# Transposing the states' exponentials by 32 by 32 blocks and a DMA instead of on TensorE, in a fused attention and SwiGLU kernel

## The chip, the cores and the metric

The kernel runs on one core of one Trainium2 chip. The metric is the device time of one execution in microseconds (us). Engines are named as the profile names them: PE is TensorE (PEld its weight loads), DVE is VectorE, ACT is ScalarE, POOL is GpSimd, SP is SyncE, whose queue issues nearly all DMAs.

## The reference, cut to what matters (softmax written short)

There are 8 batches of 8 heads; each head has 512 tokens and 32 states of width 64. Tokens read states and states read tokens, both with a softmax. All 544 rows of a batch, 512 wide over the heads, then go through an RMS norm and a SwiGLU layer of 1536 units.

```python
scores = scale * np.matmul(x, state.transpose(0, 1, 3, 2))      # 512 x 32
a = softmax(scores)                ; xread = np.matmul(a, state)
scores2 = scale * np.matmul(state, x.transpose(0, 1, 3, 2))     # 32 x 512
a2 = softmax(scores2)              ; sread = np.matmul(a2, x)
x = np.concatenate([xread, sread], axis=2)     # then (B*S, H*D) = (4352, 512)
rms = np.sqrt(np.mean(x * x, axis=-1, keepdims=True) + 1e-06)
xn = x / rms * rms_g
g = xn @ w_gate ; val = xn @ w_val
out = (g / (1 + np.exp(-g)) * val) @ w_out
```

## The kernel before, in words

Everything is float32. The kernel works batch by batch in a software pipeline. After an opening stage (batch 0, the reading of batch 1, the conversion of the weights) come seven periods, one for each of the batches 1 to 7, and a last stage for the 256 state rows of all batches.

A period does two things at once. It runs the SwiGLU layer for the 512 tokens of batch b: the hidden products (`hidden_seven`, line 674, each product in seven instead of eight block products) and the output products (`project_seven`, line 836). And it runs the attention of batch b + 1: `tokens_read` and `states_read`. The order within a period is written out by hand for PE, DVE and ACT: a string `PERIOD` has one letter for each step, a letter stands for a stream (a Python generator), and each letter emits that stream's next step. `h` are the hidden products on PE, `t` and `u` what ACT and DVE do with them; `p`, `c` and `k` are the output products, their copies by ACT and sums by DVE; `v`, `w` and `x` make the batch's own weights (line 528 on PE, ACT copies, POOL sums); `a` is `tokens_read`, `s` is `states_read`. Each engine runs its instructions in the order of the string; waits between engines follow from the data. The same string serves all seven periods. In the last, where there is no further batch, `s` is empty and `a` stands for the norm of the state rows. POOL's and SP's orders are not written by hand.

The steps that the change touches, in the order of a batch:

- `tokens_read` multiplies the softmaxed scores by the states (line 410, PE), ACT squares the four results into `sq`, three DVE additions (line 420) leave one tile `sq[:, 0]` of 128 partitions by 512 tokens. PE sums it over partitions with four products against a column of ones (line 424), DVE adds 1e-6 (line 428), POOL takes the power -0.5 (line 270), PE spreads the result along rows (line 277), DVE scales the batch's `aT_s` with it (line 434). The scaled `aT_s` and POOL's `slot_sums` of it are what the next period's first hidden products read.
- `states_read` takes the maximum of the states' scores (line 446, DVE), ACT makes the exponentials `e2` and their sums (line 452), PE transposes them in two groups of four 128 by 128 blocks (line 459), ACT copies each group from PSUM to `e2T` (line 461), and PE multiplies `e2T` with the batch's tokens (line 471). DVE divides by the sums (line 478), PE transposes the result (line 482), DVE puts it into `xsT` (line 484), which only the last stage reads.

From batch 2 on the scores themselves are already made on blocks: DVE transposes 32 by 32 blocks of the inputs (lines 329 and 335) and `x` is loaded so that this suffices. A block transpose exchanges rows and columns inside each 32 by 32 block and leaves every block within its own 32 partitions.

Three pools of PSUM tiles matter: `aps` (two buffers, named `at` in the profile) holds nearly everything of the attention, `vps` (two, `pv`) shares the own weights' products, and `fx`, `fy`, `fz` (`f`) belong to the layer's products. The tag `eS` is one SBUF buffer, held by the tokens' exponentials during the first part of a batch.

Of the kernel before, what the change touches and what calls it, by code (L numbers as in the profile page):

```python
# [8 lines left out]
F32 = mybir.dt.float32  # L9
# [3 lines left out]
ALU = mybir.AluOpType  # L13
ACTF = mybir.ActivationFunctionType
AXX = mybir.AxisListType.X
PSUM = bass.MemoryType.PSUM

P = 128
# [10 lines left out]
)  # L29

PERIOD = (
    "hhtvtvhtxhuxhuthhtuhuhtxhhhutuuuhthhuttxahhxhthuuuuuxhavuvhtxhtxhhttuauhxuxhxuut"
    "hhhtuhthutuuhuuuhhauuhtaaauxuhthautuuhhthuhuautaaphuuuapuaaaaacaasapcpaaaaaaaakp"
    "psackaauaacakkpapaakaacpsaskcsssppsasspwswkswxkxxkkpxpxccxss"
)

STATES = (
# [6 lines left out]
def kernel(  # L44
# [20 lines left out]
    nc = tc.nc  # L65
    VE, SE, GE, TE = nc.vector, nc.scalar, nc.gpsimd, nc.tensor
# [75 lines left out]
    GE.memset(bounds[:, 1:2], 255.0 * (1 << 23))  # L142
    rms_g = consts.tile([P, NI], F32, name="rms_g")


    w_d = [scratch.tile([P, NI, 2, 2, P], F32, name="w_d%d" % mp) for mp in range(NM // 2)]
    w_sb = {}
    wo = consts.tile([P, NM, DM], F32, name="wo")
    hb = consts.tile([P, NM, S], F32, name="hb")
# [117 lines left out]
    def mean_root(ss, n):  # L267

        ri = two.tile([P, NC], F32, name="ri")
        GE.tensor_tensor(out=ri[:, 0:n], in0=ss, in1=mhalf[:, 0:n], op=ALU.pow)  # L270
        return ri

    def along_rows(ri, n):

        rp = aps.tile([P, NC, P], F32, name="at")
        for c in range(n):
            TE.transpose(out=rp[:, c, :], in_=ri[:, c:c + 1].to_broadcast([P, P]), identity=ident)  # L277
        return rp.rearrange("p c t -> p (c t)")
# [4 lines left out]
    def scores(b, packed, soft):  # L283

        xb = x_sb[b]
        stT = two.tile([P, 4, Ns], F32, name="stT")
        tp = aps.tile([P, 4, Ns], F32, name="at")
        TE.transpose(out=tp.rearrange("p j n -> p (j n)"),
                     in_=packed.rearrange("p e d -> p (e d)"), identity=ident)
        yield  # L290
        VE.tensor_copy(stT, tp)
        yield "step"

        xT = one.tile([P, 4, NC, P], F32, name="xT", tag="xT")
        for c in range(NC):
            tp = aps.tile([P, 4, P], F32, name="at")
            for j in range(4):
                TE.transpose(out=tp[:, j, :], in_=xb[:, c, P * j:P * j + P], identity=ident)
            yield
            SE.copy(xT[:, :, c, :], tp)  # L300
            yield "step"


        sp = [aps.tile([P, S], F32, name="at") for e in range(2)]
        for j in range(4):
            for e in range(2):
                TE.matmul(out=sp[e][Ns * j:Ns * j + Ns, :], lhsT=stT[D * e:D * e + D, j, :],
                          rhs=xT[D * e:D * e + D, j].rearrange("p c t -> p (c t)"),
                          start=True, stop=True)
        yield  # L310


        sS = read[b] = two.tile([P, 2, NC, P], F32, name="sS")
        eS = soft["e"] = one.tile([P, 2, S // Ns, Ns], F32, name="eS", tag="eS")
        for e in range(2):
            VE.transpose(out=eS[:, e].rearrange("p k n -> p (k n)"), in_=sp[e])
            yield
            SE.copy(sS[:, e].rearrange("p c t -> p (c t)"), sp[e])
            yield "step" if e else None

        soft["st"] = stT
        soft["half"] = lambda e: eS[:, e]
        soft["back"] = lambda e: [(aT_s[b][:, e], eS[:, e].rearrange("p k n -> p (k n)"))]

    def scores_of_blocks(b, packed, soft):
# [30 lines left out]
        for g in (2, 3, 0, 1):  # L356
# [7 lines left out]
                                   eS[:, g].rearrange("p e c n -> p e (c n)"))  # L364
                                  for g in (2 * q, 2 * q + 1)]

    def tokens_read(b):
        packed, soft = rows.pop(b), {}
        yield from (scores if b < 2 else scores_of_blocks)(b, packed, soft)
        half = soft["half"]  # L370
        m1 = two.tile([P, 2, S // Ns], F32, name="m1")
        z1 = two.tile([P, 2, S // Ns], F32, name="z1")

        def along(t, e):
            return t[:, e].unsqueeze(2).to_broadcast([P, S // Ns, Ns])

        for e in range(2):
            VE.reduce_max(out=m1[:, e], in_=half(e), axis=AXX)
            yield
            VE.tensor_tensor(out=half(e), in0=half(e), in1=along(m1, e), op=ALU.subtract)  # L380
            yield
            SE.activation(out=half(e), in_=half(e), func=ACTF.Exp, scale=SCALE)
            yield "step"
        stT_g[b] = two.tile([P, 4, Ns], F32, name="stT_g")
        if b > 1:
            soft["st"] = aps.tile([P, 4, Ns], F32, name="at")
            TE.transpose(out=soft["st"].rearrange("p j n -> p (j n)"),
                         in_=packed.rearrange("p e d -> p (e d)"), identity=ident)
            yield
        VE.tensor_tensor(out=stT_g[b], in0=soft["st"], in1=rms_g.unsqueeze(2).to_broadcast([P, 4, Ns]),  # L390
                         op=ALU.mult)
        yield
        aT_s[b] = two.tile([P, 2, S], F32, name="aT_s")
        for e in range(2):
            VE.reduce_sum(out=z1[:, e], in_=half(e), axis=AXX)
            yield
            VE.tensor_scalar(z1[:, e], z1[:, e], 1e-9, None, op0=ALU.add)
            VE.reciprocal(z1[:, e], z1[:, e])
            yield
            VE.tensor_tensor(out=half(e), in0=half(e), in1=along(z1, e), op=ALU.mult)  # L400
            yield
            for to, blocks in soft["back"](e):
                VE.transpose(out=to, in_=blocks)
            yield "step"


        reads = [(aps, vps)[j // 2].tile([P, S], F32, name=("at", "pv")[j // 2]) for j in range(4)]
        for j in range(4):
            for e in range(2):
                TE.matmul(out=reads[j][D * e:D * e + D, :],  # L410
                          lhsT=packed[Ns * j:Ns * j + Ns, e, :],
                          rhs=aT_s[b][Ns * j:Ns * j + Ns, e],
                          start=True, stop=True)
        yield
        sq = one.tile([P, 4, S], F32, name="sq", tag="xT")
        for i, j in enumerate((2, 3, 0, 1)):
            SE.activation(out=sq[:, i, :], in_=reads[j], func=ACTF.Square, scale=DM ** -0.5)
            yield "step" if i == 3 else None
        for i, j in ((0, 1), (2, 3), (0, 2)):
            VE.tensor_tensor(out=sq[:, i, :], in0=sq[:, i, :], in1=sq[:, j, :], op=ALU.add)  # L420
            yield
        sp = aps.tile([P, NC], F32, name="at")
        for c in range(NC):
            TE.matmul(out=sp[:, c:c + 1], lhsT=sq[:, 0, P * c:P * c + P], rhs=ones,  # L424
                      start=True, stop=True)
        yield
        ss = two.tile([P, NC], F32, name="ss")
        VE.tensor_scalar(ss, sp, 1e-6, None, op0=ALU.add)
        yield "step"
        ri = mean_root(ss, NC)  # L430
        yield
        rp = along_rows(ri, NC)
        yield
        VE.tensor_tensor(out=aT_s[b], in0=aT_s[b],
                         in1=rp.unsqueeze(1).to_broadcast([P, 2, S]), op=ALU.mult)
        yield "step"

    def states_read(b):

        xb, sS = x_sb.pop(b), read.pop(b)  # L440
        e2 = one.tile([P, 2, NC, P], F32, name="e2")
        s2 = two.tile([P, 2], F32, name="s2")
        m2 = two.tile([P, 2], F32, name="m2")
        z2 = two.tile([P, 2], F32, name="z2")
# [4 lines left out]
        VE.tensor_scalar(s2, m2, -SCALE, None, op0=ALU.mult)  # L449
        yield  # L450
        for e in range(2):
            SE.activation(out=e2[:, e], in_=sS[:, e], func=ACTF.Exp, scale=SCALE,
                          bias=s2[:, e:e + 1], accum_out=z2[:, e:e + 1])
            yield "step" if e else None
        e2T = one.tile([P, 2, NC, P], F32, name="e2T")
        for e in range(2):
            tp = aps.tile([P, NC, P], F32, name="at")
            for c in range(NC):
                TE.transpose(out=tp[:, c, :], in_=e2[:, e, c, :], identity=ident)  # L459
            yield  # L460
            SE.copy(e2T[:, e], tp)
            yield "step"
        VE.tensor_scalar(z2, z2, 1e-9, None, op0=ALU.add)
        VE.reciprocal(z2, z2)
        yield
# [1 line left out]
        for e in range(2):  # L467
            for c in range(NC):
                for j in range(4):
                    h = 2 * j + e  # L470
                    TE.matmul(out=rp[Ns * j:Ns * j + Ns, e, :],  # L471
                              lhsT=e2T[:, e, c, Ns * j:Ns * j + Ns],
                              rhs=xb[:, c, D * h:D * h + D],
                              start=(c == 0), stop=(c == NC - 1))
        yield
# [567 lines left out]
```

## Time and profile before

| what | value |
|---|---|
| median of 5 runs (lowest to highest) | 791.63 us (790.94 to 792.32) |
| the profiled execution: its time, its span | 791.63 us, 789.8 us |
| granted TensorE clock in it | 0.998 |
| PE busy, PEld busy | 777.7 us (98%), 604.4 us (77%) |
| DVE, ACT, POOL busy | 521.7 us (66%), 334.4 us (42%), 170.8 us (22%) |
| DMA moved | 95.77 MB, mean 121 GB/s |

The profile is of one execution, whose time is also the median; 1.8 us of it lie around the span. A period, from one batch's first hidden product to the next one's, takes 85.48 us (223.83 to 309.31 us of the trace). Busy shares are means over stages with different limits. PE's busy time counts pipelined matmuls, so a busy PE is not PE at its peak; how much one matmul costs in a row of them is read from the chain of waits, where its share of the time stands without overlap.

### The profile page before, as it was taken

The numbers are of one execution on the slowest core, as the hardware profiler recorded it, in microseconds if no ns is written. First come the engines' busy times: TensorE is split into PE (matmuls) and PEld (weight loads), VectorE is DVE, ScalarE is ACT, GpSimd is POOL, SyncE is SP. The second block draws the span as 40 slices with busy tenths as digits, with TensorE's granted clock in tenths as the row PEclk, the third lists the DMA queues.
The fourth block names the chain that finished last, engine by engine and source line by source line (L and its number), as shares of the span: only waits on it lengthen the run. The fifth ranks groups of instructions, "written<-read, shape, count | busy, mean of one in ns | idle before, by whom it ended". The sixth has DMA issues, their size and how long they took to land.

```text
span 789.8 us, 13559 instructions
## 1 busy us (share of the span) xinstructions
PE 777.7 (98%) x5478; PEld 604.4 (77%) x5478; DVE 521.7 (66%) x822; ACT 334.4 (42%) x560; POOL 170.8 (22%) x216
## 2 busy tenths in 40 slices
PE   6999999999999999999999999999999999999998
PEld 5643444788878887888878887888788887888996
DVE  4999997688338951887268833895189725781461
ACT  5998864552245323542255124532353225410320
POOL 0100003430244023420433024402341043400000
PEclk9999999999999999999999999999999999999999
DMA  9888865730065005610263007500530024201311
GB/s 286 228 271 311 275 190 167 217 122 1 24 203 217 2 17 177 221 31 17 90 217 121 1 24 207 215 2 14 197 153 12 13 79 176 107 5 35 121 54 27
DMA packets 69277, 95.77 MB, mean 121 GB/s; under 512 B 46432, under 2 KB 54112, under 8 KB 62304
## 3 DMA queue, kind: packets, MB, share of 16 engines
q1 hardware_dynamic: 67040, 94.33, 36.5%
q8 instruction: 43, 0.70, 0.4%
q10 hardware_dynamic: 2176, 0.59, 0.4%
q14 instruction: 18, 0.15, 0.1%
HBM read 79.69 MB, written 15.20 MB: 120 GB/s over the span
## 4 chain that ended last, share of the span: by engine, by line
PE 93%; DVE 5%; issue 0%; DMA 0%; ACT 0%; SPq 0%
PE f L674 37%; PE f L836 35%; PE f L776 5%; PE pv L570 4%; PE at L528 3%; PE pv L528 3%; DVE ex L248 1%; PE at L471 1%; PE at L410 1%; DVE raw L244 1%; PE at L346 1%; PE at L424 1%; PE at L459 1%; DVE w_m L253 1%; PE pv L346 1%; PE at L277 0%
## 5 line engine op out<-in xcount | busy, mean ns | idle before, releaser
L836 PE MATMUL f<-wo,hb 128*128 128x256 f32 x540 | 123.4, 380 | 0.2 <-ACT ot L873 0.2
L674 PE MATMUL f<-aT_s,v 128*128 128x256 f32 x504 | 120.6, 382 | 0.0
L836 PEld LDWEIGHTS f<-wo,hb 128*128 128x128 f32 x540 | 101.4, 190 | 13.5 <-ACT ot L873 0.4
L674 PEld LDWEIGHTS f<-aT_s,v 128*128 128x128 f32 x504 | 94.1, 190 | 19.6 <-DVE c L736 5.0
L736 DVE TENSOR_TENSOR g<-g,f 128x512 f32<-128x512 f32 (+1 forms) x96 | 61.9, 653 | 68.4 <-PE f L674 63.9
L674 PE MATMUL f<-aT_t,vs 128*128 128x256 f32 x336 | 87.1, 381 | 0.0
L270 POOL TENSOR_TENSOR ri<-ss,mhalf 128x4 f32<-128x4 f32 x8 | 13.5, 1692 | 321.2 <-DVE s L449 210.9
L727 ACT ACTIVATE hb<-g 128x1024 f32<-128x1024 f32 (+1 forms) x48 | 48.2, 1005 | 79.3 <-DVE g L736 79.3
L836 PE MATMUL f<-wt,hs 128*128 128x256 f32 x360 | 81.0, 381 | 0.0
L836 PEld LDWEIGHTS f<-wt,hs 128*128 128x128 f32 x360 | 67.3, 190 | 14.1 <-issue 5.1
L674 PEld LDWEIGHTS f<-aT_t,vs 128*128 128x128 f32 x336 | 63.2, 190 | 15.0 <-issue 5.9
L873 ACT COPY ot<-f 128x256 f32<-128x256 f32 x60 | 21.4, 373 | 122.9 <-PE f L836 122.9
L554 POOL TENSOR_TENSOR vs<-v 128x256 f32<-128x256 f32 x42 | 31.4, 746 | 164.3 <-ACT v L539 164.2
L739 DVE SCALAR_TENSOR_TENSOR hb<-hb,g 128x1024 f32<-128x1024 f32 x42 | 53.2, 1267 | 4.6 <-ACT hb L727 4.6
L725 ACT COPY g<-f 128x512 f32<-128x512 f32 (+1 forms) x48 | 26.9, 561 | 55.8 <-PE f L674 55.8
L776 PE MATMUL f<-wo,hb 128*128 128x512 f32 x96 | 44.7, 600 | 0.0
L557 POOL TENSOR_TENSOR vs<-v,vs 128x256 f32<-128x256 f32 x42 | 44.4, 1056 | 0.0
L570 PE MATMUL pv<-aT_s,v 128*128 128x512 f32 x96 | 43.6, 593 | 0.0
L674 PE MATMUL f<-aT_s,vs 128*128 128x256 f32 x168 | 43.1, 379 | 0.0
L674 PE MATMUL f<-aT_t,v 128*128 128x256 f32 x168 | 43.1, 379 | 0.0
L836 PE MATMUL f<-wo,hs 128*128 128x256 f32 x180 | 41.2, 379 | 0.0
L836 PEld LDWEIGHTS f<-wt,hb 128*128 128x128 f32 x180 | 33.7, 190 | 9.4 <-DVE ot L881 5.0
(144 smaller groups left out, 1279.8 us busy)
## 6 DMA issues: line engine op xcount, KB each, us to landing
w_m<-w_d SPq DMA_DIRECT2D x48, 1024.0 KB, 6.5
out_dram<-ot SPq DMA_DIRECT2D x56, 128.0 KB, 2.1
raw<-in_moe_w_val_dram SPq DMA_DIRECT2D x6, 1024.0 KB, 5.5
raw<-in_moe_w_out_dram SPq DMA_DIRECT2D x6, 1024.0 KB, 7.9
x_b<-in_x_dram SPq DMA_DIRECT2D x96, 64.0 KB, 2.6
w_d<-w_m SPq DMA_DIRECT2D x6, 1024.0 KB, 4.9
raw<-in_moe_w_gate_dram SPq DMA_DIRECT2D x5, 1024.0 KB, 6.9
x_b<-in_x_dram SPq DMA_DIRECT2D x6, 256.0 KB, 6.7
```

The costliest lines, as they stand in the source:

```text
L528: TE.matmul(out=pv[e][Ns * j:Ns * j + Ns, :], lhsT=stT_g[b][D * e:D * e + D, j, :], rhs=w[D * e:D * e + D, j].rearrange("p m k f -> p (m k ...
L554: GE.tensor_tensor(out=vs[:, 0], in0=a21, in1=a22, op=ALU.add)
L557: GE.tensor_tensor(out=vs[:, 2], in0=a12, in1=vs[:, 1], op=ALU.subtract)
L570: TE.matmul(out=to[0], lhsT=lhs(i, k), rhs=r, start=(i == 0), stop=(i == len(rhs) - 1))
L674: TE.matmul(out=ps[:, i, 0:half], lhsT=l[:, i, :], rhs=r, start=(start and i == 0 and k == 0), stop=(k == len(lhs) - 1), skip_group_check= ...
L725: SE.copy(gates(q)[1], q["x"][:, :, 0:half])
L727: SE.activation(out=hb[:, 2 * mp:2 * mp + 2, 0:n].rearrange("p m (c t) -> p m c t", c=2), in_=q["g"][:, :, :, 0:half], func=ACTF.Silu if s ...
L736: VE.tensor_tensor(out=to, in0=to, in1=q[ps][:, :, 0:half], op=ALU.add)
L739: VE.scalar_tensor_tensor(out=h, in0=h, scalar=1.0, op0=ALU.add, op1=ALU.mult, in1=q["g"].rearrange("p m c t -> p m (c t)"))
L776: TE.matmul(out=banks[r], lhsT=hb[:, m, P * r:P * r + P], rhs=wo[:, m, :], start=(m == 0), stop=(m == NM - 1))
L836: TE.matmul(out=banks[name][:, r, :], lhsT=lhs(k)[:, P * r:P * r + P], rhs=rhs(k), start=(start and r == 0 and k == 0), stop=(k == HM - 1) ...
L873: SE.copy(to, banks[name][:, r, :])
```

## The change

For batches 0 and 1 the arithmetic and its order stay. For batches 2 to 7:

- `states_read`: the two groups of TensorE transposes and the two ACT copies go. ACT writes the exponentials in another layout, DVE transposes all of them by 32 by 32 blocks in one instruction into `eB` (which takes the buffer with tag `eS`), a DMA from ScalarE's queue writes `eB` to a scratch tensor in HBM (512 KB), and four DMAs from the same queue read it back into `e2T`, 128 KB into 32 partitions each, which moves the blocks between partition groups.
- `tokens_read`: the four products with ones go. DVE transposes the summed squares by blocks, sums each block's rows (one `reduce_sum`, 128 by 16 results), PE finishes the sum with one product against a constant `groups` of zeros and ones (128 by 128, 16 columns), and four small DVE instructions, one for each 32 partitions, add 1e-6.
- `groups` is built by 16 small POOL instructions at the start; the small tile `stT` of batches 0 and 1 has one buffer instead of two.
- `PERIOD` is written anew, for all seven periods: 224 letters instead of 220.

Two places in the new order on PE differ beyond the removed steps. The own weights' products of pairs 4 and 5, which stood next to each other (`v` twice), are now apart, with four steps of `h` products between. And line 471's product, which stood ahead of the next batch's two weight products (`w`), now follows them and stands between the last two output products.

```diff
-    "hhtvtvhtxhuxhuthhtuhuhtxhhhutuuuhthhuttxahhxhthuuuuuxhavuvhtxhtxhhttuauhxuxhxuut"
...
+    "hhvtvhtthuxhxhhuhtutuhhxttuxhhuuuxhthuauhuthhtuxthhuhuhuhvhtttuhuhxhxavutuuhahtx"
...
+    groups = consts.tile([P, 4, Ns], F32, name="groups")
...
+    e_d = [scratch.tile([4, Ns, 4, 8 * Ns], F32, name="e_d%d" % k) for k in range(2)]
...
-        stT = two.tile([P, 4, Ns], F32, name="stT")
+        stT = one.tile([P, 4, Ns], F32, name="stT")
...
+    def rms_on_blocks(b, sq):
+        n = S // Ns
+        VE.transpose(out=sq[:, 1, :], in_=sq[:, 0, :])
+        yield
+        part = one.tile([P, n], F32, name="part")
+        VE.reduce_sum(out=part, in_=sq[:, 1, :].rearrange("p (k f) -> p k f", f=Ns), axis=AXX)
+        yield
+        sp = aps.tile([P, n], F32, name="at")
+        TE.matmul(out=sp, lhsT=groups.rearrange("p i t -> p (i t)"), rhs=part,
+                  start=True, stop=True)
+        yield
+        ss = two.tile([P, NC], F32, name="ss")
+        for g in range(4):
+            VE.tensor_scalar(ss[Ns * g:Ns * g + Ns], sp[Ns * g:Ns * g + Ns, g::4], 1e-6, None,
+                             op0=ALU.add)
+        yield "step"
...
+        rp = yield from (rms_on_array if b < 2 else rms_on_blocks)(b, sq)
...
+            eB = one.tile([P, 4, 2, NC, Ns], F32, name="eB", tag="eS")
+            VE.transpose(out=eB.rearrange("p g e c n -> p (g e c n)"),
+                         in_=e2.rearrange("p g e c t -> p (g e c t)"))
+            yield
+            nc.scalar.dma_start(out=e_d[b % 2].rearrange("j t g f -> (j t) (g f)"),
+                                in_=eB.rearrange("p g e c n -> p (g e c n)"))
+            yield
+            for g in range(4):
+                nc.scalar.dma_start(out=e2T[Ns * g:Ns * g + Ns].rearrange("t j e c n -> t j (e c n)"),
+                                    in_=e_d[b % 2][:, :, g].rearrange("j t f -> t j f"))
+                yield
```

More of the change, by code (lines that the diff above doesn't have):

```diff
@@ L31 @@
 PERIOD = (
-    "hhtvtvhtxhuxhuthhtuhuhtxhhhutuuuhthhuttxahhxhthuuuuuxhavuvhtxhtxhhttuauhxuxhxuut"
-    "hhhtuhthutuuhuuuhhauuhtaaauxuhthautuuhhthuhuautaaphuuuapuaaaaacaasapcpaaaaaaaakp"
-    "psackaauaacakkpapaakaacpsaskcsssppsasspwswkswxkxxkkpxpxccxss"
+    "hhvtvhtthuxhxhhuhtutuhhxttuxhhuuuxhthuauhuthhtuxthhuhuhuhvhtttuhuhxhxavutuuhahtx"
+    "xuhtthuhxhhthuuaxuhuuhuuhttthhauhtuahuuupuuatuaauahuuuaapaaaaaaaaaaappaacapcapak"
+    "ascsupakaaaakascpcaspaackakssasppakkakpssssawwksxwpxxxsspxkxcssc"
 )
@@ L143 @@
     rms_g = consts.tile([P, NI], F32, name="rms_g")
+    groups = consts.tile([P, 4, Ns], F32, name="groups")
+    for i in range(4):
+        GE.tensor_copy(groups[:, i], ident[:, 0:Ns])
+        for j in range(1, 4):
+            GE.tensor_tensor(out=groups[:, i], in0=groups[:, i],
+                             in1=ident[:, Ns * j:Ns * j + Ns], op=ALU.add)
     w_d = [scratch.tile([P, NI, 2, 2, P], F32, name="w_d%d" % mp) for mp in range(NM // 2)]
+    e_d = [scratch.tile([4, Ns, 4, 8 * Ns], F32, name="e_d%d" % k) for k in range(2)]
     w_sb = {}
@@ L365, in scores_of_blocks, with rms_on_array @@
                                   for g in (2 * q, 2 * q + 1)]
+    def rms_on_array(b, sq):
+        sp = aps.tile([P, NC], F32, name="at")
+        for c in range(NC):
+            TE.matmul(out=sp[:, c:c + 1], lhsT=sq[:, 0, P * c:P * c + P], rhs=ones,
+                      start=True, stop=True)
+        yield
+        ss = two.tile([P, NC], F32, name="ss")
+        VE.tensor_scalar(ss, sp, 1e-6, None, op0=ALU.add)
+        yield "step"
+        ri = mean_root(ss, NC)
+        yield
+        rp = along_rows(ri, NC)
+        yield
+        return rp
+    def rms_on_blocks(b, sq):
[7 more added lines that the diff above has]
+        TE.matmul(out=sp, lhsT=groups.rearrange("p i t -> p (i t)"), rhs=part,
+                  start=True, stop=True)
+        yield
+        ss = two.tile([P, NC], F32, name="ss")
+        for g in range(4):
+            VE.tensor_scalar(ss[Ns * g:Ns * g + Ns], sp[Ns * g:Ns * g + Ns, g::4], 1e-6, None,
+                             op0=ALU.add)
+        yield "step"
+        ri = mean_root(ss, NC)
+        yield
+        rp = along_rows(ri, NC)
+        yield
+        return rp
     def tokens_read(b):
@@ L421, in tokens_read @@
             yield
[L422 to L433, printed above, removed]
+        rp = yield from (rms_on_array if b < 2 else rms_on_blocks)(b, sq)
         VE.tensor_tensor(out=aT_s[b], in0=aT_s[b],
@@ L440, in states_read @@
         xb, sS = x_sb.pop(b), read.pop(b)
-        e2 = one.tile([P, 2, NC, P], F32, name="e2")
+        e2 = one.tile([P, 4, 2, NC, Ns], F32, name="e2")
+        exps = e2.rearrange("p g e c t -> p (g e c t)").rearrange("p (e c s) -> p e c s", e=2, s=P)
         s2 = two.tile([P, 2], F32, name="s2")
@@ L451, in states_read @@
         for e in range(2):
-            SE.activation(out=e2[:, e], in_=sS[:, e], func=ACTF.Exp, scale=SCALE,
+            to = e2[:, :, e].rearrange("p g c t -> p c g t")
+            if b < 2:
+                to = exps[:, e]
+            SE.activation(out=to, in_=sS[:, e].rearrange("p c (g t) -> p c g t", t=Ns)
+                          if b > 1 else sS[:, e], func=ACTF.Exp, scale=SCALE,
                           bias=s2[:, e:e + 1], accum_out=z2[:, e:e + 1])
             yield "step" if e else None
[L455 to L459, printed above, removed]
-            yield
-            SE.copy(e2T[:, e], tp)
-            yield "step"
+        e2T = one.tile([P, 4, 2, NC, Ns], F32, name="e2T")
+        if b < 2:
+            flat = e2T.rearrange("p j e c n -> p (j e c n)").rearrange("p (e c s) -> p e c s", e=2, s=P)
+            for e in range(2):
+                tp = aps.tile([P, NC, P], F32, name="at")
+                for c in range(NC):
+                    TE.transpose(out=tp[:, c, :], in_=exps[:, e, c, :], identity=ident)
+                yield
+                SE.copy(flat[:, e], tp)
+                yield "step"
+        else:
+            eB = one.tile([P, 4, 2, NC, Ns], F32, name="eB", tag="eS")
+            VE.transpose(out=eB.rearrange("p g e c n -> p (g e c n)"),
+                         in_=e2.rearrange("p g e c t -> p (g e c t)"))
+            yield
+            nc.scalar.dma_start(out=e_d[b % 2].rearrange("j t g f -> (j t) (g f)"),
+                                in_=eB.rearrange("p g e c n -> p (g e c n)"))
+            yield
+            for g in range(4):
+                nc.scalar.dma_start(out=e2T[Ns * g:Ns * g + Ns].rearrange("t j e c n -> t j (e c n)"),
+                                    in_=e_d[b % 2][:, :, g].rearrange("j t f -> t j f"))
+                yield
         VE.tensor_scalar(z2, z2, 1e-9, None, op0=ALU.add)
@@ L471, in states_read @@
                     TE.matmul(out=rp[Ns * j:Ns * j + Ns, e, :],
-                              lhsT=e2T[:, e, c, Ns * j:Ns * j + Ns],
+                              lhsT=(e2T[:, j, e, c, :] if b > 1 else
+                                    flat[:, e, c, Ns * j:Ns * j + Ns]),
                               rhs=xb[:, c, D * h:D * h + D],
```

## The prediction

> **What bounds the kernel now.** I read the chain of waits first, then the chain of one period in order of time, then the stages' busy times and the DMA table. The page's chain by engine:
>
> ```profile
> PE 93%; DVE 5%; issue 0%; DMA 0%; ACT 0%; SPq 0%
> ```
>
> The DVE share lies before 62 us, where weights are converted. Every period afterwards is a gapless chain of PE pieces, and all repeat at 85.48 us (223.83 to 309.31). The end of one, from the chain in order of time (start, length, what):
>
> ```profile
> 283.82 4.53 PE f L836 x21
> 288.35 0.79 PE at L424 x8
> 289.13 2.70 PE f L836 x12
> 291.83 0.44 PE at L277 x4
> 292.27 0.44 PE at L459 x4
> 292.70 5.18 PE f L836 x24
> 297.89 0.44 PE at L459 x4
> 298.32 2.59 PE f L836 x12
> 300.92 1.03 PE at L471 x64
> 301.95 1.02 PE pv L528 x16
> 302.97 0.86 PE at L528 x16
> 303.82 5.38 PE f L836 x24
> ```
>
> Lengths here are PE's own time, without overlap, so a step's removal gives back exactly its length as long as PE keeps finding its inputs ready. Note also that the same work costs more after a small step: 24 instructions of L836 take 5.18 us after transposes and 5.38 after L528.
>
> The other engines have room there. The stage of that stretch (us, busy of PE, PEld, DVE, ACT, POOL, clock, DMA share, GB/s):
>
> ```profile
> 285.00:309.20 24.20, 24.20 (x206) 20.15 (x205) 7.18 (x17) 5.82 (x14) 9.34 (x12) 1.00 0.29 86
> ```
>
> **What PE loses.** L459: two groups at 0.44, 0.88 us. L424: 0.79 us for 8 instructions. Together 1.67 us a period, in the six periods that prepare batches 2 to 7.
>
> **What PE gains.** The one product with `groups` is two instructions of L424's weight shape (128 by 128), with 16 columns instead of one: at L424's 0.79 / 8 = 0.10 each, 0.20 us. The trace has no 16-column product. The bounds are 0.20 and 0.22 (L459's transposes, 128 columns, 0.44 / 4 = 0.11 each), so its size is not the question. The 0.11 us that L836 pays after L424 (2.70 for 12 against 2.59) I leave, since `groups` stands in the same sort of place.
>
> The new order adds two changes between large and small steps. What one costs, from the chain at the start of batch 1's layer, where single steps stand between each other:
>
> ```profile
> 138.00 1.02 PE at L528 x16
> 139.02 1.06 PE f L674 x4
> 140.09 1.02 PE pv L528 x16
> 141.10 0.86 PE at L528 x16
> ```
>
> The second L528 of a pair takes 0.86, one that follows a large product 1.02; four L674 after an L528 take 1.06 where they take 0.86 after their own kind. Before, pairs 4 and 5 of the own weights shared one entry and one exit; apart, they pay 0.16 + 0.20 = 0.36 us more, in all seven periods. L471 moves out of its place ahead of L528 (which pays 1.02 there as it does behind L674) to between two output products: the exit, 0.20 us, is paid once more, in six periods. The Trainium skill has a rule that speaks against the change here: TensorEngine Tiling (Array Packing), Key Properties, says that a change of tiling mode makes the array finish what is in it first. It names no time, and the rows above price it.
>
> Sum for a period with attention: 1.67 - 0.20 - 0.36 - 0.20 = 0.91 us saved, six times 5.46; the seventh period pays 0.36. Net 5.1 us.
>
> **What moves to other engines, and whether it stays hidden.** I laid the new order's steps after L410 on PE's time, by the lengths above, from the period's start. L410 ended at 59.14 (282.97); with the 0.36 it ends at 59.5. Two output products (5.38) to 64.9, one to 67.5, `groups` to 67.7, one to 70.4, one to 73.0, L277 to 73.4, one to 76.0, the two weight products to 77.9, one to 80.7, L471 to 81.7, the last to 84.5, L482: 84.6, which is 85.48 - 0.91 again.
>
> Squares: ACT's four squares end 2.2 us after L410 (282.97 to 285.15), 61.7, DVE's last addition about 1.5 later, 63.2. The added block transpose (0.70, by L329's 128x512) and block sum (0.66, L395) come to 64.6; PE asks for them at 67.5. The four additions are 0.16 each, 0.64 instead of 0.16, and POOL's power 1.74: 68.0 + 0.6 + 1.7 = 70.3 against L277 at 73.0. If this cover of 2.7 us were gone, the excess would be paid on PE six times.
>
> Exponentials: the second is queued on ACT behind a copy that needs an output product's end at 64.9, so it ends near 66.2 (copy 0.37, exponential 0.72, its sum 0.19). DVE's transpose of 1024 columns is L335's 1.24 us: 67.5. DVE's additions come behind it and are those counted above from 68.0. The DMA's wait blocks ACT; behind it in ACT's order stand only the other DMAs and the copies of the next weights, due at 77. The two ACT copies that go (0.58 each, L461) were off the path and bring nothing.
>
> The DMAs, none of this shape in the trace, are bounded by these rows (KB each, us from issue to landing):
>
> ```profile
> w_d<-w_m SPq DMA_DIRECT2D x6, 1024.0 KB, 4.9
> out_dram<-ot SPq DMA_DIRECT2D x56, 128.0 KB, 2.1
> x_b<-in_x_dram SPq DMA_DIRECT2D x96, 64.0 KB, 2.6
> fours<-in_state_dram SPq DMA_DIRECT2D x24, 64.0 KB, 6.9
> ```
>
> The write of 512 KB lies between the 256 KB store's 3.0 us (`hs`) and 4.9: I take 3.9. Issued at 67.8, it lands at 71.7. ACT then issues four reads at SP's spacing of 0.6 us (15 `x` pieces in 9.27), the last by 74.2; by the 2.6 row they land at 76.8. L471 wants them at 80.7: 3.9 us to spare. DMA is quiet in that part (share 0.01 in 267 to 285 us). `fours`, 6.9 us, runs behind megabyte loads, and I take it for the bad end: 67.8 + 4.9 + 2.5 + 6.9 = 82.1, 1.4 us late. By the Trainium skill (DMA: Bandwidth & Descriptors, Anatomy of one DMA: about 2 us fixed, mostly until the target confirms, plus bytes at 436 GB/s, measured on another issuing path) the estimate is 3.2 and 2.3 us, which lands at 75.8. No run here shows that path.
>
> First half of the period: the new order puts DVE's and ACT's steps a little elsewhere, with the same work. The tightest waits are PE's on ACT's copies: a copy (L720, 0.59, and some 0.2 to start) has two hidden products of 0.86 to hide behind, 0.9 us of slack, in both orders. A new one is the second pair of output products, which needs two DVE steps of 0.68 after the last hidden product; one output product (2.59) covers them, 1.0 us of slack. Other edits cost nothing: 16 small POOL instructions at the start, when POOL has nothing due until 32 us; the single `stT`, whose last reader in batch 0 (L390) ends at 18.3 us while the second copy comes after 36.8.
>
> Total: 791.63 - 5.1 = 786.5 us; the profiled execution's time is the median, so both bases agree.
>
> **Rivals.** First, the changes of step cost nothing where PE can load weights ahead; the saving is then 6 x (1.67 - 0.20) = 8.8 us, 782.8. For it: after transposes (L459) L836 pays nothing. Against: every L528 and L410 exit in the trace pays 0.19 to 0.20. Second, the carried exponentials come late, and PE, in order, stands at L471 with the last output product behind it. From 3.9 us beyond my chain on each us costs six; from 0.91 us late on the change loses. At the bad end, 1.4 us late: 786.5 + 8.4 = 794.9. Against it: the quiet DMA there. Third, the rewritten first half or the longer DVE chain loses about 0.9 us a period in one of the waits with that much slack: 786.5 + 6 x 0.9 = 791.9, no change. Against it: the added 3.1 us of DVE (1.24 + 0.70 + 0.66 + 3 x 0.16) stand in a stage where DVE is busy 7.18 of 24.2. That the change does not do what it says is ruled out by the built order: each of six periods has eight transposes fewer, and one product where four with one column stood.
>
> **How the numbers follow.** My forecast (785 to 788) 0.62; no cost of changing 0.12; late exponentials 0.13; a lost 0.9 us 0.09; a mixture that still gains 0.04. The measurement can tell 0.2%, 1.6 us, from no change. Faster: 0.62 + 0.12 + 0.04 = 0.78; same 0.09; slower 0.13. The range from 782.5 takes in the first rival, and up to 792.0 the third; late exponentials, 0.13, lie above it.
>
> **What would show it.** Right: a period of 84.6 us; L836 or L674 of 1.06 per four after each single L528; no wait of PE on a DMA at L471's product; `e2T` landing 3 to 4 us before it. Wrong: idle time of PE before that product or before L277, reads that take over 6 us, ACT held in its DMA wait while a copy for PE is due, or periods of 84.0 us.

## The result: 793.85 us, slower by 0.25%

| | median (lowest to highest) |
|---|---|
| before | 791.66 us (790.93 to 792.35, 45 runs) |
| changed | 793.85 us (792.85 to 794.15, 25 runs) |
| ratio | 1.0025, 95% interval 1.002 to 1.003 |

The prediction was 786.5 us, with a range to 792.0 and 0.78 on faster. It was wrong: the time lies outside the range and on the other side. The profiled execution of the changed kernel has a span of 791.9 us, 2.1 more than before, at a granted clock of 1.0. In its lines L896 is the old L836 (output products), L734 the old L674 (hidden products), L588 the old L528 (own weights), L530 the old L471 (product with the carried exponentials), L285 the old L277, L542 the old L482; L401 is the new product with `groups`, L933 ACT's copies of output halves.

The page's chain has gained ACT, which stood at 0% before:

```profile
PE 92%; DVE 6%; ACT 1%; issue 1%; DMA 0%; SPq 0%
```

A period now takes 85.72 us (224.21 to 309.93) instead of 85.48. The chain of its end, in order of time, from where L458, the old L410, is done (start, length, what):

```profile
283.70 5.39 PE f L896 x24
289.09 0.02 issue
289.12 0.38 ACT ot L933
289.50 0.04 issue
289.54 2.87 PE f L896 x12
292.41 0.02 issue
292.44 0.38 ACT ot L933
292.82 0.04 issue
292.86 5.45 PE f L896 x24
...
303.21 2.79 PE f L896 x12
306.00 1.03 PE at L530 x64
307.03 2.79 PE f L896 x12
```

Twice PE stands still for 0.44 us (0.02 + 0.38 + 0.04) until ACT has copied half of a PSUM bank, and restarts slowly: 2.87 for 12 instructions that take 2.59 in a row, 5.45 for 24 that take 5.18. TensorE's waits say the same (in total, times, longest):

```profile
PE f L896 <- ACT ot L933: 5.0, 13, 0.5
```

Two a period in six periods and one in the last make 13; the one in the last stood in the kernel before as well (`717.73 0.38 ACT ot L873` in its chain). Of the product with `groups` nothing is seen in the chain, because it runs inside the second wait.

What the two copies wait for can be read in the kernel before as well. Its ACT instructions in order of time, with the idle time before each and what ended it:

```profile
288.38 0.37 ACT L873 COPY ot<-f 128x256 f32<-128x256 f32 x1 [2.96 <-PE f L836]
291.87 0.37 ACT L873 COPY ot<-f 128x256 f32<-128x256 f32 x1 [1.55 <-PE f L836]
```

The first copies the half that had been finished 2.7 us earlier (it is the first of two products of 2.69 that end at 288.35), yet it starts only when the second is done; the other starts at the end of the next product (291.83), which writes the first half. So the two halves of a bank (they are one tile of the program, `f`, 2 by 256 columns) count as one thing: a copy waits for the last product into the bank before it in the order of `PERIOD`, and the next product into the bank waits for the copy. Before, the steps that stood between were L424 (0.79 us) in the first place, and L277 with the first group of transposes (0.44 + 0.44) in the second. Each was longer than the copy. The change took out the four products with ones and the transposes and moved L277 (now L285) two output products on; with them went the cover.

### The profile page after: what moved, and what is told of

Read it like the earlier page. It is cut to its first block, busy times and chain, and to the rows that moved or that the text cites. A ratio compares the mean times of both kernels' runs of the same rounds, so it can differ in the third digit from the quotient of the medians.

```text
span 791.9 us, 13483 instructions
## 1 busy us (share of the span) xinstructions
PE 775.1 (98%) x5394; PEld 592.4 (75%) x5394; DVE 549.1 (69%) x858; ACT 328.3 (41%) x548; POOL 178.7 (23%) x232
## 4 chain that ended last, share of the span: by engine, by line
PE 92%; DVE 6%; ACT 1%; issue 1%; DMA 0%; SPq 0%
PE f L734 38%; PE f L896 35%; PE f L836 5%; PE pv L630 3%; PE at L588 3%; PE pv L588 3%; DVE ex L256 1%; DVE raw L252 1%; PE at L530 1%; PE at L458 1%; PE at L354 1%; DVE w_m L261 1%; ACT ot L933 1%; DVE top L249 1%; PE pv L354 1%
## 5 line engine op out<-in xcount | busy, mean ns | idle before, releaser
L896 PE MATMUL f<-wo,hb 128*128 128x256 f32 x540 | 124.2, 382 | 5.0 <-ACT ot L933 5.0
L734 PE MATMUL f<-aT_s,v 128*128 128x256 f32 x504 | 120.6, 382 | 0.0
L896 PEld LDWEIGHTS f<-wo,hb 128*128 128x128 f32 x540 | 101.4, 190 | 21.4 <-ACT ot L933 8.2
L734 PEld LDWEIGHTS f<-aT_s,v 128*128 128x128 f32 x504 | 94.1, 190 | 19.6 <-issue 7.2
L734 PE MATMUL f<-aT_t,vs 128*128 128x256 f32 x336 | 87.1, 382 | 0.0
L896 PE MATMUL f<-wt,hs 128*128 128x256 f32 x360 | 81.0, 381 | 0.0
L896 PEld LDWEIGHTS f<-wt,hs 128*128 128x128 f32 x360 | 67.3, 190 | 14.1 <-issue 5.1
L933 ACT COPY ot<-f 128x256 f32<-128x256 f32 x60 | 21.0, 375 | 129.9 <-PE f L896 129.9
L734 PEld LDWEIGHTS f<-aT_t,vs 128*128 128x128 f32 x336 | 63.1, 190 | 15.2 <-issue 6.2
L599 ACT COPY v<-pv 128x512 f32<-128x512 f32 x42 | 22.7, 592 | 58.2 <-PE pv L588 49.2
L836 PE MATMUL f<-wo,hb 128*128 128x512 f32 x96 | 44.7, 600 | 0.0
L734 PE MATMUL f<-aT_t,v 128*128 128x256 f32 x168 | 43.8, 383 | 0.0
L734 PE MATMUL f<-aT_s,vs 128*128 128x256 f32 x168 | 43.1, 379 | 0.0
L896 PE MATMUL f<-wt,hb 128*128 128x256 f32 x180 | 42.4, 386 | 0.0
```

The source lines that it names most:

```text
L734: TE.matmul(out=ps[:, i, 0:half], lhsT=l[:, i, :], rhs=r, start=(start and i == 0 and k == 0), stop=(k == len(lhs) - 1), skip_group_check= ...
L836: TE.matmul(out=banks[r], lhsT=hb[:, m, P * r:P * r + P], rhs=wo[:, m, :], start=(m == 0), stop=(m == NM - 1))
L896: TE.matmul(out=banks[name][:, r, :], lhsT=lhs(k)[:, P * r:P * r + P], rhs=rhs(k), start=(start and r == 0 and k == 0), stop=(k == HM - 1) ...
L933: SE.copy(to, banks[name][:, r, :])
```

## The experiments

The theory, A: PE waits for ACT's copies of the bank of `x` that the removed steps had covered. The rival, B: PE is simply busier than computed, through entries and exits of small steps and slow restarts.

**More work in the second gap.** In `rms_on_blocks`:

```diff
-        TE.matmul(out=sp, lhsT=groups.rearrange("p i t -> p (i t)"), rhs=part,
-                  start=True, stop=True)
+        for again in range(3):
+            TE.matmul(out=sp, lhsT=groups.rearrange("p i t -> p (i t)"), rhs=part,
+                      start=True, stop=True)
```

> The changed kernel, with the product with the constant groups made three times instead of once (same operands, same result): 4 more TensorE instructions, some 0.4 us of PE time, in each of six periods, between two output products. Theory A (PE waits there for ACT's copies of the same PSUM bank, 0.44 us each time, and the steps that the change removed had been covering those waits): the added work runs inside the wait, so the time stays between 793.5 and 794.5 us. Theory B (no wait of that sort matters; PE is simply busy longer, by entries and exits of small steps and slower restarts): six times 0.4 is added, 796.2 us.

Measured: 793.55 us, 1.0024 of before (1.0015 to 1.0033), the same as the change. In the chain the second wait is gone, and work stands in its place (7 waits of the output products on ACT are left of 13; every line number is one higher here):

```profile
289.68 2.86 PE f L897 x12
292.53 0.57 PE at L402 x6
293.11 5.33 PE f L897 x24
```

0.57 us of work and a restart of 5.33 instead of a wait of 0.44 and one of 5.45: four more instructions a period on the engine that bounds the kernel cost nothing. B, which asked for 796.2 us, is out.

**Another order of the output products.** In `project_seven`, for the 512-token batches, and the letters of `PERIOD` from L410's successor on:

```diff
-            yield from product("x", A(1, 0), B(0, 1))
-            yield from product("z", S_, B(1, 1))
+            if R > 1:
+                yield from product("z", S_, B(1, 1))
+            yield from product("x", A(1, 0), B(0, 1))
+            if R == 1:
+                yield from product("z", S_, B(1, 1))
...
-    "ascsupakaaaakascpcaspaackakssasppakkakpssssawwksxwpxxxsspxkxcssc"
+    "ascsupakkkaaaaascpkssaaaksccpasaappasssspakkwwksxwpxxxsspxkxcssc"
```

> The changed kernel, with another order of the output products for the 512-token batches: the two products into z's bank (states' sums times block 11) stand ahead of the two into x's bank that follow the copied sum, and both ACT copies of that bank (u2) are emitted ahead of them, so one whole output product of 2.59 us lies between the copies' earliest start and the first product that overwrites the bank. DVE's and ACT's steps are moved to suit; the same instructions otherwise. Theory A: each period loses the two waits (0.88) and the two slow restarts (2.87 and 5.45 instead of 2.59 and 5.18, 0.55) and pays for the groups product in the open (0.2 and 0.1 to restart): 1.1 us less, six times, and some 0.5 in the last period, so 786.6 us (786.0 to 787.5). Theory B: the order of these products does not matter, 793.0 to 794.5.

Measured: 785.87 us, 0.9926 of before (0.9914 to 0.9939), 8.0 us below the change, where A said 7.3 (7.6 below it, if the median of each is set against that of the kernel before beside it, 791.32 and 791.66). Three output products run in one row, none of them waits for ACT any more, and the product with `groups` shows its own price:

```profile
282.09 7.97 PE f L896 x36
290.06 0.13 PE at L401 x2
290.18 5.28 PE f L896 x24
```

**The same order in the kernel before**, with the same edit of `project_seven` and the letters of its own string moved in the same way.

> The kernel before, with the same new order of the output products and of the copies. Theory A: there the copies were already covered by the four products with ones (0.79 us) and by L277 and the first group of transposes (0.88), so only the last period, which has neither, gains some 0.5: 791.0 to 791.7 us. A rival to A, that the new order is a gain by itself, whatever lies between: about 6 us off this one too, 785.5.

Measured: 791.22 us, 0.9995 (0.9986 to 1.0004): no difference that can be told. The order is worth nearly 8 us only where the cover is missing; it is not a gain by itself.

**By the bank or by the half?** Only the two letters `c` are moved in the changed kernel's string, each directly behind the product that finishes its half:

```diff
-    "ascsupakaaaakascpcaspaackakssasppakkakpssssawwksxwpxxxsspxkxcssc"
+    "ascsupakaaaakasccpascpaakakssasppakkakpssssawwksxwpxxxsspxkxcssc"
```

> The changed kernel in its own order of products; only the two ACT copies of the half sums u2 are emitted earlier, each directly behind the output product that finishes its own half of the PSUM bank (the first between the two halves' products). If the waits hold by half of the bank, both copies now lie beside a product of the other half and the waits go: 1.0 to 1.1 us off six periods, 787.3 us. If they hold by the bank, the product of the second half must wait for the copy of the first, and the next one for the copy of the second: the same two waits, one product earlier, and the product with groups no longer runs inside one of them (0.1 to 0.25 us more a period): 794 to 795.5 us.

Measured: 794.52 us, 1.0041 (1.0029 to 1.0054). The waits have moved one product ahead, and the first now stands between the two halves:

```profile
282.93 2.80 PE f L896 x12
...
285.76 0.38 ACT ot L933
...
286.18 2.87 PE f L896 x12
...
289.08 0.38 ACT ot L933
```

So the waits hold by the bank as a whole, not by its halves. The two halves are also one tile of the program, and no run here parts the two: whether two tiles in one bank would wait for each other in the same way is open. They are waits that the program carries; a version without them was not tried, since two engines would then use one bank unguarded. That is what the Trainium skill warns of (PSUM — Partial Sum Buffer, PSUM bank collisions raise a hardware error): guard PSUM by bank and group of 32 partitions, not by address. The trace shows only that the program guards no finer than the bank, with 0.44 us a wait; what happens without the guard no run here shows.

**Each half of the change, with the waits covered.** First the pair of own weights' products is put together again (one `v` moved), which also prices that split:

```diff
-    "hhvtvhtthuxhxhhuhtutuhhxttuxhhuuuxhthuauhuthhtuxthhuhuhuhvhtttuhuhxhxavutuuhahtx"
+    "hhvtvhtthuxhxhhuhtutuhhxttuxhhuuuxhthuauhuthhtuxthhuhuhuhvvhtttuhuhxhxautuuhahtx"
```

> As e2_order, and the own weights' products of pairs 4 and 5 next to each other again (one letter of the period's order moved). Theory A with the price of a change of step as predicted (0.36 us for the split pair, seven periods): 2.5 us below e2_order, 784.1 us. If the changes of step cost nothing, equal to e2_order.

Measured: 784.79 us, 0.9912 (0.9898 to 0.9926), 1.1 below e2_order where 2.5 was expected. The period is 84.32 against 84.49. The entry and exit are saved, but one product's weights are now loaded late, behind an addition by DVE (weight loads of PE in order of time):

```profile
250.88 0.73 PEld L734 LDWEIGHTS f<-aT_t,v 128*128 128x128 f32 x4 [0.32 <-DVE c L796]
```

On that base the squares went back to TensorE (`rp = yield from rms_on_array(b, sq)`, two letters `a` fewer), and in another kernel the transposes (the branch of `b < 2` taken by all batches, with the old layout of `e2`, two letters `s` fewer and one moved):

> As e4_order_join, but the squares are summed on TensorE again, as before, in all batches (four products with ones instead of DVE's block transpose, block sum and one product with groups); only the states' exponentials go by blocks and DMA. With the waits covered by the order, TensorE's own time should count in full: 0.79 against the 0.13 that the product with groups took in e2_order, 0.66 us more in six periods, 4.0 us above e4_order_join: 788.8 us. If the freed TensorE time is still lost in some wait, it stays near 784.8.

> As e4_order_join, but the states' exponentials are transposed on TensorE again, as before, in all batches (two groups of four transposes and two ACT copies instead of a block transpose, a write and four reads); only the squares go by blocks. With the waits covered, 0.88 us more in six periods, 5.3 us above e4_order_join: 790.1 us. If the DMA round trip costs something that shows nowhere as a wait, less than that.

Measured: 788.88 us (0.9966, 0.9953 to 0.9978) and 789.73 us (0.9976, 0.9966 to 0.9985). Against e4_order_join the squares are worth 4.1 us and the states' transposes 4.9, where 4.0 and 5.3 were computed from the lengths in the chain. The 0.4 us that the second lacks is no cost of the DMAs: with the transposes back, the chain has 0.48 and 0.44 us for them, but the output products behind take 5.18 again where they took 5.28 directly behind `groups`, so 0.82 us a period, 4.9 in six. Once nothing waits, PE's removed time is given back in full, and a cost of the DMA round trip cannot be seen.

**The product with the carried exponentials, nearer and too early.** Two more kernels move its letter `s`; both also put DVE's late addition (a `u`) ahead of the block transpose (an `a`):

```diff
-    "hhvtvhtthuxhxhhuhtutuhhxttuxhhuuuxhthuauhuthhtuxthhuhuhuhvvhtttuhuhxhxautuuhahtx"
-    "xuhtthuhxhhthuuaxuhuuhuuhttthhauhtuahuuupuuatuaauahuuuaapaaaaaaaaaaappaacapcapak"
-    "ascsupakkkaaaaascpkssaaaksccpasaappasssspakkwwksxwpxxxsspxkxcssc"
+    "hhvtvhtthuxhxhhuhtutuhhxttuxhhuuuxhthuauhuthhtuxthhuhuhuhvvhtttuhuhxhxautuuhuaht"
+    "xxhtthuhxhhthuuaxuhuuhuuhttthhauhtuahuuupuuatuaauahuuuaapaaaaaaaaaaappaacapcapak"
+    "ascsupakkkaaaaascpkssaaaksccpasaappasssspakkwwksxwspxxxspxkxcssc"
```

That is e5_order_join_rp against e4_order_join; e8_rp_early has a third line that puts two letters `s` ahead of the `p`:

```diff
-    "ascsupakkkaaaaascpkssaaaksccpasaappasssspakkwwksxwspxxxspxkxcssc"
+    "ascsupakkkaaaaascpkssaaaksccpasaappasssssspakkwwkxwpxxxspxkxcssc"
```

> As e4_order_join, and two letters moved. The product with the carried exponentials (line 530) stands directly behind the next batch's two weight products, so that it shares their exit to the large products: 0.20 us less in six periods by the prediction's price. And DVE's addition into c of pair 3 stands ahead of the second block transpose of x instead of behind it, because in e4_order_join the product behind that addition had its weights loaded 0.3 us late: 0.17 us less in seven periods. Expected from 784.8: 784.8 - 1.2 - 1.2 = 782.4 us. The carried exponentials land some 3 us before they are needed there (read off e4_order_join's trace). If the changes between large and small steps cost nothing, only the second term remains, 783.6; if the DMAs are on the path, it is slower than 784.8.

Measured: 784.32 us, 0.9909 (0.9893 to 0.9924), not 782.4. The late load is gone, but the exit was not shared: the built order drew the next period's first hidden product in between, and it pays the 0.20 (1.06 instead of 0.86):

```profile
299.63 1.06 PE f L734 x4
300.69 1.03 PE at L530 x64
```

A period takes 84.13 us, 0.19 less than in e4_order_join, which is the late load alone (48 instructions of L734 behind the pair take 10.56 us instead of 10.74); e10 below mends nothing but that load.

> As e5_order_join_rp, but the product with the carried exponentials is asked for about 4.5 us earlier, behind the spreading of the norms (line 285) and ahead of the second product of that pair, which is some 1.6 us before the reads land in e4_order_join's trace. This prices the rival of late DMAs: PE should wait there for the reads, 1.6 us and a restart in each of six periods, 10 us above e5_order_join_rp (792 to 794). If the reads do not bind, it equals e5_order_join_rp or is 1 us above it.

Measured: 799.88 us, 1.0102 (1.0088 to 1.0117), 15.6 us above e5_order_join_rp, where 10 was expected. Here PE does wait for the carried exponentials, and where it does not, for the PSUM buffer that DVE still reads (waits of PE):

```profile
PE at L530 <- DMA e2T<-e_d: 7.1, 4, 2.1
PE at L530 <- DVE aT_s L471: 2.8, 2, 1.5
```

These waits are 9.9 of the 15.6 us. Another 5.2 stand behind them: in all six periods the second product with the own weights takes 1.72 us instead of 0.86. So late exponentials, the prediction's second rival, do cost PE's time where they are late. In the change they are not. In the period shown the four reads were issued from 297.49 on, the last at 298.8, and took 2.8 to 4.2 us, so all had landed by 303.0, and L530 asks at 306.00. The least room is in the period in which the write took 4.5 us: its last read landed by 389.5 (issued at 386.4, at most 3.1 us), and L530 asks at 391.7.

**The best version found**: e4_order_join with that addition moved, and nothing else.

> As e4_order_join, with the one letter moved that e5 moved besides: DVE's addition into c of pair 3 ahead of the second block transpose of x. The late weight load (0.17 us) goes from seven periods: 1.2 us below e4_order_join, 783.6 us. If the load was late for another reason, equal to e4_order_join, 784.8.

Measured: 783.02 us, 0.9892 (0.9876 to 0.9907): 8.5 us faster than the kernel before it ran beside, and faster than both kernels of this case. Its period is 84.13 us, the same as e5_order_join_rp's; the 1.3 us between the medians of those two lie within their intervals.

## Why the prediction was wrong, point by point

**The step that failed** is the layout of the new order after L410: "Two output products (5.38) to 64.9, one to 67.5, `groups` to 67.7, one to 70.4". It took PE's own time for all there is, since "Every period afterwards is a gapless chain of PE pieces", and asked of each added step whether it stayed hidden. It did not ask what the removed steps had hidden: two waits for ACT's copies, put at nothing, which cost 0.44 us each and a slow restart. The chain before had a sign of it. In the last period, which has neither the four products with ones nor the transposes, PE stands still from 717.71 to 718.15 for a copy out of the same bank (`717.73 0.38 ACT ot L873`); with the other order (e3) that wait is gone. The working even has ACT's copy in it ("queued on ACT behind a copy that needs an output product's end at 64.9"), but as a delay of the exponentials, not as something that the next output product waits for. The stretch was to take 25.1 us from L410's end (59.5 to 84.6) and took 26.23 (283.70 to 309.93). The difference: two waits of 0.44, two slower restarts (2.87 for 2.59, 5.45 for the 5.29 of the working), less the 0.20 for `groups`, which ran in a wait: 0.88 + 0.28 + 0.16 - 0.20 = 1.12. Six times that is 6.7 of the 7.35 us by which the prediction missed. Of the rest, 0.17 is in the last period (17.63 for a row of hidden products that takes 17.46 elsewhere) and 0.13 before the first, both of open cause; 0.11 is what the median lies above the profiled execution (793.74), and some 0.2 is rounding (a period took 85.72 where the sum, unrounded, gives 84.57: 1.15 too much, not 1.12).

**"A step's removal gives back exactly its length as long as PE keeps finding its inputs ready"** stands, and the condition was the point: e6 and e7 price what comes back at 4.1 and 4.9 us. Behind L410 the condition was tested for DVE, POOL and the DMAs, and for ACT's copies only in the first half (L720), not for the bank behind the removed step. The third rival had the right size (0.9 us a period) and the wrong places.

**The price of a change of step** was right in kind. The first half of the period ran 59.49 us to L410's end, 59.5 forecast, with the split's 0.36 in it; L530's two neighbours take 2.79 each where before the undivided pair took 5.38 behind L528. The measured joining (1.1 us) is less because of the late load; with that mended (e10) it is 2.9 below e2_order, 2.5 computed. The first rival, that changes cost nothing, is out. The Trainium skill's rule (TensorEngine Tiling (Array Packing), Key Properties: a change of mode makes the array drain) agrees with the 1.06 behind each single small step.

**The block sums and the DMAs** held, with less room than forecast. Squares were summed in time (PE did not wait at L401), and POOL ended at 297.22, 1.1 us before L285 at 298.31, where 2.7 was forecast. One reading of the working was wrong: the second exponential stands not behind the copy that waits for 64.9, but behind the next one (292.44). It ended 69.3 us into the period instead of 66.2, and the write was issued at 70.6 instead of 67.8. The share of 0.01 given for a quiet DMA is that of 267 to 285 us, ahead of the write's place; where the write and the reads were to stand, 288 to 300.6 us in the kernel before, the share is at most 0.16. The DMAs:

```profile
e_d<-eB ACTq DMA_DIRECT2D x6, 512.0 KB, 2.6
e2T<-e_d ACTq DMA_DIRECT2D x24, 128.0 KB, 3.2
```

I had 3.9 for the write and 2.6 for the reads, 6.5 together; it was 5.8. The Trainium skill's formula (DMA: Bandwidth & Descriptors, Anatomy of one DMA; measured on another issuing path) gives an estimate of 3.2 and 2.3, 5.5 together, too long for the write and too short for the reads. The exponentials had 2.2 to 3.8 us to spare in the six periods of the change, where 3.9 was forecast.

**The product with `groups`** was put at 0.20 us and takes 0.13 in the open (e2_order), with the 0.10 of restart that was left in.

## What to carry to other kernels

When work is taken off the bounding engine, look for what else ran in its time: list every instruction of another engine that starts at the end of the step before and ends before the step behind, and ask who waits for it. A copy out of PSUM that starts within 0.03 us of a matmul's end, while the bound engine does something small, is such a thing, and it costs nothing in the profile until the small step goes. Where a bank is both copied out and written again, let work into another bank stand between, not the small steps that happen to be there.

## What the runs showed of the hardware that was not expected

Two halves of one PSUM bank, here also one tile, are not independent for the program's waits: with the copy placed between the halves' products the second product stood still 0.44 us (e9). A write of 512 KB from 128 partitions to HBM lands in 2.6 to 2.7 us in five of the six periods, in which nothing else of size moved beside it (204 GB/s over 2.57 us is its own 512 KB), no more than the 256 KB store's 2.7 in the same trace; in the sixth, where other transfers ran beside it (179 GB/s over 4.45 us is some 270 KB more), it took 4.5; the four reads of 128 KB into 32 partitions each take longer, 3.2 us, than 128 KB stores with 1.8.
